# Widening the recurrence's narrow matrix products from 54 or 40 to 64 moving columns

## The chip, the cores and the metric

The kernel runs on one core of a Trainium2 chip. The metric is the device time of one execution in microseconds (us). TensorE (PE in the profile) multiplies a stationary block of up to 128x128 (loaded by LDWEIGHTS, PEld in the profile) with a stream of moving columns; VectorE (DVE), ScalarE (ACT) and GpSimd (POOL) do the rest; SyncE (SP) issues most transfers. TensorE's clock has two levels here, 1.2 and 2.4 GHz; the profile gives the granted clock as a share of the upper one.

## The reference

Three parts follow each other: a recurrence over 768 steps, a mixture of experts, and a dense feed-forward layer. Only the first is touched:

```
for t in range(768):          # for each of 4 x 8 (batch, head), D = 40
    y[t]  = r[t] @ state
    Sa    = state @ a[t]                                   # over e
    state = state * w[t] (over e) - outer(Sa, b[t]) + outer(v[t], k[t])
```

Then x = y as 3072 tokens of 320; each token goes to one of 8 experts (320 to 1024 to 320, relu), and then all tokens through 320 to 2048 to 320 with h * sigmoid(1.702 h).

## The kernel before, in words

**The recurrence** (class Attn) is cut into 24 chunks of 32 steps. The 128 partitions hold 4 batches of 32 steps; the 8 heads lie beside each other in two groups g of four heads. Within a chunk the dependence on earlier steps is solved with matrices made ahead (`ahead`: `decays`, `early`, `solve`), so that a chunk is a chain of products: `chain` builds W from G times v, then U from T times W, V from N times X, U again from T times V; then the new state from k times v and b times U (`outer`) and the old state (`pos`); `state` splits and spreads the state, `output` makes the chunk's Y.

All products are in fp16 with each operand as a high and a low half, three products for one (`mm3`: high-high, low-high, high-low). A head has 40 columns. The operands lie so that several halves or heads follow each other in a row, and a product may read on beyond its 40 columns; the columns of its result beyond 40 are never read. `WIDE` (line 1286) is how many columns most products stream: 54. Two kinds stream 40: those of U into the state (`outer` with k=1, line 1637), and the last of four heads in `times` (line 1672), behind which the tile ends. `v` and `U` rows hold a head as 128 columns: high, low, high again, 8 zeros. `parts` (line 1661) makes the high and low half of W, X and V as tiles of 2 halves x 4 heads x 40 with two buffers for each name.

**The order of work** of the recurrence, and of some of the experts' preparation, is written by a planner (class Plan): every operation is collected with its predecessors, given a cost, and the planner simulates the engines several times forward and backward, keeps its shortest plan, and emits each engine's instructions in that order; it also chooses VectorE or ScalarE for the operations that may run on either (`either`). A product of m columns costs max(m / 2.0, 25) ns there (20 for the smallest), so 27 ns for 54 columns, 25 for 40 and 32 for 64. All instructions that the planner issues carry one line, L234. Engines run their instructions strictly in that order.

**After the recurrence** (from about 545 us) come the experts (lines L870, L884 and others) and, from about 760 us, the dense layer (L1154, L1178).

Of the kernel before, what the change touches and what calls it, by code (L numbers as in the profile page):

```python
# [468 lines left out]
F16 = mybir.dt.float16  # L469
# [25 lines left out]
class Mlp:  # L495
# [265 lines left out]
    def tables2(self):  # L761
# [13 lines left out]
        sq = [128, NE, NE]  # L775
        outer = lambda t: t.rearrange("p (j o) -> p j o", o=1).to_broadcast(sq)
        nc.vector.tensor_tensor(le, one(end[:, 1:]).to_broadcast(sq), outer(end[:, 1:]), op=ALU.is_le)
        nc.vector.tensor_reduce(after, le, axis=AX.X, op=ALU.add)
        nc.vector.tensor_scalar(after, after, NE - 1.0, None, op0=ALU.min)
# [503 lines left out]
RING = 3  # L1283
PX, MX, MGX, SSB, V16B, UEB, SDB, PN = 4, 2, 2, 1, 2, 1, 2, 3
AHEAD = 1500
WIDE = 54
AT = ((0,), (1,), (2, 3), ())
SK, SA, SV, SS = 2.0 ** 10, 2.0 ** 6, 2.0 ** 8, 2.0 ** 12
WMIN, WMAX = 0.8, 1.0
# [3 lines left out]
def sub(t, off, dims):  # L1293

    a = t if isinstance(t, bass.AP) else t[:, :]
    return bass.AP(a.tensor, a.offset + off, [list(a.ap[0])] + [list(d) for d in dims])


class Attn:
# [7 lines left out]
    def __init__(self, tc, ctx, W, AB, KVR, keep, lent):  # L1307

        self.tc = tc
        nc = self.nc = self.plan = Plan(tc)  # L1310
# [71 lines left out]
        for k in (8, 10):  # L1382
            t = self.neg[k] = cp.tile([128, 128], F16, name=f"neg{k}")
# [7 lines left out]
        for b2 in range(2):  # L1391
            for j in range(3):
                r = slice(64 * b2, 64 * b2 + 64)
# [7 lines left out]
        nc.vector.memset(self.wb[:, 0:1], WMIN)  # L1401
        nc.vector.memset(self.wb[:, 1:2], -WMAX)
        self.M, self.C, self.E, self.N = {}, {}, {}, {}

    def _zero(self, name, shape):
        t = self.cp.tile(shape, F16, name=name)
        names = " ".join("abcd"[:len(shape) - 1])
        self.clear(t.rearrange(f"p {names} -> p ({names})"))
        return t
# [156 lines left out]
    def bd(self, dst, src, hs):  # L1566

        for b in range(4):
            o, m = dst[:, :, hs, 32 * b:32 * b + 32], self.own[:, b:b + 1]
            self.nc.either(("vector", "tensor_scalar", (o, src, m, None), dict(op0=ALU.mult)),  # L1570
                           ("scalar", "activation", (o, src, AF.Copy), dict(scale=m)))
# [62 lines left out]

    def outer(self, out, k, x, g, first, last):

        w = 40 if k else WIDE
        for n, (a, o) in enumerate(((0, 0), (1, 0), (0, 40))):
            for i in range(4):
                for bp in range(2):  # L1640
                    r = slice(64 * bp, 64 * bp + 64)
                    self.nc.tensor.matmul(out[:, bp, i, 0:w], lhsT=self.KB[r, k, 4 * g + i, a, :],
                                          rhs=x[r, 4 * g + i, o:o + w], start=first and n + i == 0, stop=last and n + i == 5)

    def chain(self, c, g):
        nc = self.nc
        M, C = self.M[c // 4], self.C[c]
        hs = slice(4 * g, 4 * g + 4)
        U, B = self.Ust, C["B"]
        hl = lambda t, h: (t[:, h, 0:WIDE], t[:, h, 40:40 + WIDE])  # L1650
        bd = lambda t, h: (t[:, 0, h, :], t[:, 1, h, :])
        W = self.pw.bank([4, 64], f"w{g}")
        self.mm3([(W[:, i, :], bd(self.Gbd, 4 * g + i), hl(C["v"], 4 * g + i)) for i in range(4)], True, c == 0)
        if c:
            for i in range(4):
                h = 4 * g + i
                for b in range(4):
                    s = slice(32 * b, 32 * b + 32)
                    nc.tensor.matmul(W[s, i, 0:40], lhsT=C["aE"][0:120, h, s], rhs=self.Ss[g][0:120, b // 2, b % 2, i, :],
                                     start=False, stop=(i == 3))  # L1660
        def parts(x, k, tag):

            t = self.p2.tile([128, 2, 4, 40], F16, tag=tag, bufs=V16B)
            x = x[:, :, 0:40]
            nc.scalar.activation(t[:, 0], x, AF.Copy, scale=2.0 ** -k)
            nc.tensor.matmul(x, lhsT=self.neg[k], rhs=t[:, 0], start=False, stop=True, skip_group_check=True)
            nc.scalar.activation(t[:, 1], x, AF.Copy, scale=2.0 ** -k)
            return t

        def times(out, st, x, first, **k):  # L1670
            f = x.rearrange("p a h e -> p a (h e)")
            self.mm3([(out[:, i, :], bd(st, 4 * g + i), [f[:, a, 40 * i:min(40 * i + WIDE, 160)] for a in range(2)])
                      for i in range(4)], first, True, **k)

        W16 = parts(W, 8, "W16")
        Up = self.pw.bank([4, 64], f"w{g}")
        times(Up, self.Tbd, W16, True)
        X16 = parts(Up, 8, "X16")
        V = self.pw.bank([4, 64], "v")
        times(V, self.Nbd, X16, True)  # L1680
        V16 = parts(V, 10, "V16")
        nc.tensor.matmul(Up[:, :, 0:40], lhsT=self.pos8, rhs=X16[:, 0], start=False, stop=False, skip_group_check=True)
        times(Up, self.Tbd, V16, False, skip_group_check=True)
        Up = Up[:, :, 0:40]
        self.twice(U[:, hs, :], Up, 80, 2.0 ** -10)
        nc.tensor.matmul(Up, lhsT=self.neg[10], rhs=U[:, hs, 0:40], start=False, stop=True, skip_group_check=True)
        nc.scalar.activation(U[:, hs, 40:80], Up, AF.Copy, scale=2.0 ** -10)
        if g:
            UE = C["UE"] = self.p2.tile([128, 8, 128], F16, tag="UE", bufs=UEB)
            nc.sync.dma_start_transpose(out=UE, in_=U.rearrange("p h x -> p (h x)"))  # L1690
        if c < NCH - 1:
            Sp = self.ps.tile([128, 2, 512], F32, tag="s")[:, :, 0:256].rearrange("p a (h x) -> p a h x", h=4)
            for bp in range(2 if c else 0):
                for j in range(2):
                    nc.tensor.matmul(Sp[:, bp, :, 0:WIDE], lhsT=self.pos, rhs=self.S16[g][:, bp, :, 40 * j:40 * j + WIDE],
                                     start=(j == 0), stop=False)
            self.outer(Sp, 0, C["v"], g, c == 0, False)
            self.outer(Sp, 1, U, g, False, True)
            S = self.S32[g]
            P = self.M[(c + 1) // 4]["P"][:, (c + 1) % 4, :, hs]  # L1700
            nc.vector.tensor_tensor(S, Sp[:, :, :, 0:40],
                                    P.rearrange("p a (h o) -> p a h o", o=1).to_broadcast([128, 2, 4, 40]), op=ALU.mult)
        C["next"] = c < NCH - 1
# [22 lines left out]
    def output(self, c, Sd, Y):  # L1726
        nc = self.nc
        M, C = self.M[c // 4], self.C[c]
        U, B = self.Ust, C["B"]
        hl = lambda t, h: (t[:, h, 0:WIDE], t[:, h, 40:40 + WIDE])  # L1730
        bd = lambda t, h: (t[:, 0, h, :], t[:, 1, h, :])
# [58 lines left out]
    def range(self, keep, ones, ps):  # L1790

        nc = self.nc
        v = keep.tile([128, 6], F16, name="gv")
        t = keep.tile([128, 1], F32, name="gt")
        g = keep.tile([128, 1], F32, name="gg")
        self.held = keep.tile([128, 1], F32, name="held")
        nc.vector.tensor_reduce(t, self.viol, axis=AX.X, op=ALU.add)
        nc.vector.tensor_scalar(v[:, 0:1], t, 0.0, None, op0=ALU.is_equal)
        nc.vector.tensor_scalar(v[:, 1:6], self.mag, MAGMIN, None, op0=ALU.is_ge)
        nc.tensor.matmul(ps[:, 0:6], lhsT=ones, rhs=v, start=True, stop=True)  # L1800
        nc.vector.tensor_reduce(t, ps[:, 1:6], axis=AX.X, op=ALU.min)
        nc.vector.tensor_scalar(g, ps[:, 0:1], 128.0, None, op0=ALU.is_equal)
        nc.vector.tensor_scalar(self.held, t, 1.0, g, op0=ALU.is_ge, op1=ALU.mult)
# [144 lines left out]
```

## Time and profile before

| | us |
|---|---|
| median of 3 runs | 1115.99 |
| lowest, highest | 1109.04, 1117.01 |
| profiled execution, its own time | 1107.79 |
| its span, first to last instruction | 1106.0 |

The span is 1.8 us shorter than the time of the same execution. Rows of windows give, for a stretch of the span, each engine's busy time with the count of its instructions, the granted TensorE clock, the DMA engines' busy share and GB/s. Busy times of PE include the way through the array, so matmuls in a row overlap.

### The profile page before, as it was taken

To read this page: it belongs to the slowest core of one execution; us is meant where nothing else is said; L and a number is where in the kernel's file an instruction comes from. 1 tells how busy PE (TensorE), PEld (TensorE's weight loads), DVE (VectorE), ACT (ScalarE), POOL (GpSimd) and SP (SyncE) were. 2 spreads that over 40 slices of the span, in tenths; PEclk is the share of its full clock that TensorE was granted. 3 is DMA by queue.
4 is the path that set the end of the run, shared out by engine and by line. 5 is a ranking of instruction groups with operands and counts; after the bars stand their busy time and mean duration, and the time that the engine had idled before them with its cause. 6 is when DMAs were issued, how large, how long until landed. Compare 5 with 4: busy or idle time off the path is not lost. (4 is left out here: it accounts for less than half of the span.)

```text
span 1106.0 us, 36977 instructions
## 1 busy us (share of the span) xinstructions
PE 903.8 (82%) x15537; PEld 664.9 (60%) x15537; DVE 858.8 (78%) x2089; ACT 673.9 (61%) x1468; POOL 138.8 (13%) x224
## 2 busy tenths in 40 slices
PE   0167886877778787787768998998999999999995
PEld 0155665666666665675657877885555555555553
DVE  8998998998999889887764788676766666666652
ACT  4477998998899899776722363344343434343432
POOL 2000000020020020011132223213002111111101
PEclk9999897987677678667889998999999999999998
DMA  3669789689979779758527678665011111111100
GB/s 111 128 147 182 142 157 177 115 165 193 177 148 180 127 150 172 132 104 135 157 87 201 151 198 282 149 136 128 7 25 49 30 42 35 39 36 42 38 1 25
DMA packets 250654, 129.91 MB, mean 117 GB/s; under 512 B 234400, under 2 KB 237728, under 8 KB 249312
## 3 DMA queue, kind: packets, MB, share of 16 engines
q1 hardware_dynamic: 244464, 98.09, 48.4%
q0 software_dynamic: 6000, 29.23, 7.7%
q8 instruction: 125, 2.05, 0.8%
q14 instruction: 65, 0.53, 0.2%
HBM read 57.78 MB, written 12.16 MB: 63 GB/s over the span
## 5 line engine op out<-in xcount | busy, mean ns | idle before, releaser
L1160 ACT ACTIVATE sg<-t 128x512 f32<-128x512 f32 x96 | 60.5, 630 | 184.3 <-DVE t L1158 174.3
L1154 PE MATMUL h<-xT,WH 128*128 128x512 f16 x480 | 119.3, 379 | 1.8 <-DVE g L1164 1.8
L1178 PE MATMUL acc<-OH,gh 128*128 128x320 f16 x384 | 114.8, 299 | 1.0 <-ACT gh L1166 1.0
L1178 PE MATMUL acc<-OH,gl 128*128 128x320 f16 x384 | 114.8, 299 | 0.6 <-DVE gl L1170 0.6
L1178 PE MATMUL acc<-OL,gh 128*128 128x320 f16 x384 | 114.8, 299 | 0.0
L1158 DVE TENSOR_TENSOR t<-h,sB 128x512 f32<-128x512 f32 x96 | 66.2, 690 | 52.3 <-PE h L1154 49.0
L870 PE MATMUL h<-xT,split 128*128 128x128 f16 x1536 | 96.8, 226 | 11.4 <-DVEq L916 3.9
L870 PEld LDWEIGHTS <-split 128*128 128x128 f16 x1536 | 93.1, 101 | 15.2 <-DVEq L916 4.8
L1178 PEld LDWEIGHTS <-gh 128*128 128x128 f16 x768 | 74.8, 98 | 44.3 <-ACT gh L1166 1.6
L1170 DVE TENSOR_TENSOR gl<-g,gh 128x512 f16<-128x512 f32 x96 | 66.4, 691 | 43.8 <-ACT gh L1166 39.7
L234 POOL DMA_INDIRECT XD<-XR,desti x24 | 30.9, 1289 | 480.8 <-ACT ust L234 207.0
L884 PE MATMUL y<-split,hh 128*128 128x320 f16 x384 | 83.5, 303 | 5.6 <-DVEq L969 4.7
L1154 PE MATMUL h<-xT,WL 128*128 128x512 f16 x288 | 77.8, 379 | 0.0
L1154 PEld LDWEIGHTS <-WH 128*128 128x128 f16 x480 | 46.6, 98 | 44.8 <-DVE g L1164 3.5
L234 PE MATMUL w<-s,pick 128*128 128x160 f16 x368 | 63.4, 290 | 10.0 <-DVE s L234 2.9
L234 PEld LDWEIGHTS <-kb 64*128 64x128 f16 x2208 | 46.7, 101 | 37.6 <-issue 28.1
L234 PEld LDWEIGHTS <-tbd 128*128 128x128 f16 x1152 | 51.4, 105 | 23.9 <-issue 12.1
L1164 DVE SCALAR_TENSOR_TENSOR g<-h,sg 128x512 f32<-128x512 f32 x96 | 65.4, 681 | 0.0
L1166 ACT CAST gh<-g 128x512 f16<-128x512 f32 x96 | 59.3, 617 | 1.4 <-DVE g L1164 1.4
L884 PE MATMUL y<-split,hl 128*128 128x320 f16 x192 | 58.1, 303 | 0.0
L1186 POOL DMA_INDIRECT out<-o,ti x24 | 23.5, 978 | 273.0 <-ACT o L1184 269.6
L872 ACT ACTIVATE hh<-h 128x512 f16<-128x512 f32 x48 | 28.4, 595 | 46.0 <-PE h L870 39.0
(346 smaller groups left out, 2368.3 us busy)
## 6 DMA issues: line engine op xcount, KB each, us to landing
K<-in_KVR SPq DMA_DIRECT2D x24, 480.0 KB
raw<-in_AB SPq DMA_DIRECT2D x13, 640.0 KB
s<-in_wi SPq DMA_DIRECT2D x12, 512.0 KB
s<-in_wo SPq DMA_DIRECT2D x10, 512.0 KB
raw<-in_WU SPq DMA_DIRECT2D x6, 660.0 KB
YS<-ys SPq DMA_DIRECT2D x24, 160.5 KB
Sd<-s SPq DMA_TRANSPOSE x46
raw<-in_KVR SPq DMA_DIRECT2D x1, 480.0 KB
```

Source lines behind the costliest of these rows:

```text
L234: r = self.made[i] = getattr(getattr(self.nc, e), op)(*a, **k)
L870: nc.tensor.matmul(h[:, f4, :], lhsT=a, rhs=b, start=(j == 0), stop=(j == 7))
L872: nc.scalar.activation(hh[:, s, :], h, AF.Relu)
L884: nc.tensor.matmul(y, lhsT=a[:, f, :], rhs=V(b, f), start=(n == 0), stop=(n == 23))
L1154: nc.tensor.matmul(h3, lhsT=a, rhs=r, start=(j == 0), stop=(j == 7))
L1158: nc.vector.tensor_tensor(t, hs[k], self.xs[steps[k][0]]["sB"], op=ALU.mult)
L1160: nc.scalar.activation(sgs[k], t, AF.Sigmoid, scale=1.702)
L1164: nc.vector.scalar_tensor_tensor(gs[k], hs.pop(k), 2.0 ** -4, sgs.pop(k), op0=ALU.mult, op1=ALU.mult)
L1166: nc.scalar.copy(ghs[k], gs[k])
L1170: nc.vector.tensor_tensor(gls[k], gs.pop(k), ghs[k], op=ALU.subtract)
L1178: nc.tensor.matmul(accs[c], lhsT=a[:, s], rhs=r[:, f, :], start=(f == 0 and j == 0), stop=(f == NF - 1 and j == 2))
L1186: sent.append(nc.gpsimd.indirect_dma_start(out=out, out_offset=bass.IndirectOffsetOnAxis(ap=X["ti"][:, c:c + 1], axis=0), in_=o, in_offset ...
```

## The change

`WIDE` becomes 64. In `outer`, U's products stream 64 columns too: the products with the high half now read U's second copy of it (from column 80 of the head on) and run on into the next head's columns, cut to 48 where the group of four heads ends. In `parts` each half gets a tail of 24 zeros, written once per buffer, so that the last head of `times` can stream 64 columns as well. The results that are read are the same columns as before.

```
-WIDE = 54
+WIDE = 64
...
+        self.ended = set()
...
     def outer(self, out, k, x, g, first, last):
-        w = 40 if k else WIDE
-        for n, (a, o) in enumerate(((0, 0), (1, 0), (0, 40))):
+        x = x.rearrange("p h x -> p (h x)")
+        for n, (a, o) in enumerate(((0, 80 * k), (1, 80 * k), (0, 40))):
             for i in range(4):
+                u = 128 * (4 * g + i)
+                w = min(WIDE, 512 * (g + 1) - u - o)
                 for bp in range(2):
                     r = slice(64 * bp, 64 * bp + 64)
                     self.nc.tensor.matmul(out[:, bp, i, 0:w], lhsT=self.KB[r, k, 4 * g + i, a, :],
-                                          rhs=x[r, 4 * g + i, o:o + w], start=first and n + i == 0, stop=last and n + i == 5)
+                                          rhs=x[r, u + o:u + o + w], start=first and n + i == 0, stop=last and n + i == 5)
...
         def parts(x, k, tag):
-            t = self.p2.tile([128, 2, 4, 40], F16, tag=tag, bufs=V16B)
+            t = self.p2.tile([128, 2, 160 + WIDE - 40], F16, tag=tag, bufs=V16B)
+            if t.name not in self.ended:
+                self.ended.add(t.name)
+                nc.vector.memset(t[:, :, 160:], 0.0)
+            t = t[:, :, 0:160].rearrange("p a (h e) -> p a h e", h=4)
...
         def times(out, st, x, first, **k):
-            f = x.rearrange("p a h e -> p a (h e)")
-            self.mm3([(out[:, i, :], bd(st, 4 * g + i), [f[:, a, 40 * i:min(40 * i + WIDE, 160)] for a in range(2)])
+            self.mm3([(out[:, i, :], bd(st, 4 * g + i), [sub(x[:, a, i, :], 0, [[1, WIDE]]) for a in range(2)])
                       for i in range(4)], first, True, **k)
```

## Rows read from the trace of the kernel before

**Rows 1.** The page: the span in 40 slices, busy tenths and clock tenths.
```profile
DVE  8998998998999889887764788676766666666652
PEclk9999897987677678667889998999999999999998
```
**Rows 2.** Windows: the recurrence, the experts, the dense layer.
```profile
70.00:545.00 475.00, 374.68 (x10875) 304.91 (x10878) 425.83 (x1218) 410.79 (x980) 35.05 (x49) 0.78 0.87 156
545.00:760.00 215.00, 188.64 (x2407) 160.42 (x2392) 157.90 (x353) 88.56 (x170) 51.30 (x68) 0.96 0.64 167
760.00:1106.00 346.00, 329.94 (x1964) 191.21 (x1964) 210.68 (x371) 139.78 (x262) 46.56 (x74) 0.98 0.13 33
```
**Rows 3.** Windows, sum: the 22 stretches of 70 to 545 us at clock 0.50.
```profile
sum 204.82, PE 170.47 PEld 140.73 DVE 174.04 ACT 168.03 POOL 15.98; mean PE 7.75 PEld 6.40 DVE 7.91 ACT 7.64 POOL 0.73
```
**Rows 4.** Windows, sum: the 24 stretches of 70 to 545 us at clock 1.00.
```profile
sum 270.18, PE 204.21 PEld 164.18 DVE 251.79 ACT 242.76 POOL 19.07; mean PE 8.51 PEld 6.84 DVE 10.49 ACT 10.11 POOL 0.79
```
**Rows 5.** Windows, PE alone: 4 us ahead of each of 21 falls of the clock.
```profile
104.97:108.97 4.00, 1.44 (x46) 1.00 1.31 237
...
241.51:245.51 4.00, 3.22 (x105) 1.00 0.55 170
...
sum 84.00, PE 49.24; mean PE 2.34
```
**Rows 6.** Windows, PE alone: 4 us ahead of each of 21 rises.
```profile
193.72:197.72 4.00, 4.00 (x67) 0.50 0.51 96
...
sum 84.00, PE 80.86; mean PE 3.85
```
**Rows 7.** Waits of DVE for PE, 70 to 545 us (us, times, longest), first and last.
```profile
DVE mx L234 <- PE g L234: 7.3, 7, 1.4
...
DVE xbd L234 <- PE y L234: 0.2, 1, 0.2
```
**Rows 8.** Waits of ACT for PE, 70 to 545 us, first and last.
```profile
ACT ust L234 <- PE w L234: 6.7, 10, 1.5
...
ACT V L234 <- PE r L234: 0.2, 1, 0.2
```
**Rows 9.** Timeline, PE (start, length, kind, count); 230 and 355 us at clock 0.50.
```profile
180.18 0.48 PE L234 MATMUL s<-vst,kb 64*128 64x54 f16 x24
180.50 0.45 PE L234 MATMUL s<-ust,kb 64*128 64x40 f16 x24
...
230.59 1.28 PE L234 MATMUL y<-kst,xbd 128*128 128x54 f16 x24
...
355.50 0.71 PE L234 MATMUL w<-s,pick 128*128 128x160 f16 x4
...
356.15 0.58 PE L234 MATMUL s<-ust,kb 64*128 64x40 f16 x24
...
417.82 0.77 PE L234 MATMUL y<-kst,xbd 128*128 128x54 f16 x24
...
548.35 1.33 PE L234 MATMUL w<-aE,split 128*128 128x128 f16 x21
```
**Rows 10.** Groups by line and shape: products that the change touches, and one of 128 columns.
```profile
L234 PE MATMUL s<-s,pos 128*128 128x216 f16 x176 | 36.7, 317 | 6.2 <-DVE S L234 4.3 <-issue 1.7
L234 PE MATMUL s<-ust,kb 64*128 64x40 f16 x1104 | 31.2, 187 | 8.4 <-issue 3.6 <-ACT ust L234 3.1 <-ACT kb L234 0.7
L234 PE MATMUL y<-kst,xbd 128*128 128x54 f16 x576 | 28.0, 200 | 1.3 <-ACT xbd L234 0.9 <-DVE Y L234 0.2
L234 PE MATMUL w<-V,tbd 128*128 128x40 f16 x144 | 23.6, 187 | 0.0
...
L234 PE MATMUL w<-aE,split 128*128 128x128 f16 x128 | 11.0, 219 | 0.2 <-ACT aE L234 0.2
```
**Rows 11.** Groups of DVE: small clears.
```profile
L234 DVE MEMSET kst<- 128x32 uint32 x3 | 0.3, 85 | 0.0
```
**Rows 12.** Waits of PE, 540 to 765 us, the longest.
```profile
PE t L932 <- DMA xg<-XD,xrow: 6.5, 1, 6.5
```

## The prediction

> **What bounds the kernel now.** I first read the clock over the span, then the three stages, then the stage that the change touches by clock level, then who waits for PE. The page's slices show the upper clock nearly everywhere from the experts on, and tenths of 6 to 9 before that [rows 1]. The recurrence takes 475 of 1106 us; in it DVE is busy for 425.8 us (90%), ACT for 410.8 (86%), PE for 374.7 with its pipeline's latency counted in, at a mean granted clock of 0.78 [rows 2]. So DVE and ACT fill this stage together, and PE sits between them: its products cost time where DVE or ACT stands and waits for one. Behind the recurrence the longest wait of PE is for a gather of the tokens that the recurrence sent out [rows 12]; I take what the recurrence saves or loses to move the end one for one.
>
> Split by level: 204.8 us lie at 1.2 GHz, with DVE busy 174.0 (85.0%) and ACT 168.0 (82.0%) [rows 3]; 270.2 us lie at 2.4 GHz, with DVE 251.8 (93.2%) and ACT 242.8 (89.8%) [rows 4]. A microsecond at the low level thus gets 8.2% less DVE work done. DVE waited for PE for 22.8 us in all (13 rows, the first and the last in [rows 7]), ACT for 32.4 us (16 rows, [rows 8]). 22.8 us is the most that a PE without any delay could give through DVE.
>
> Ahead of a fall of the clock PE was busy for 2.34 of 4 us on average, between 1.44 and 3.22 over 21 falls [rows 5]; ahead of a rise for 3.85 of 4 [rows 6]. So the low stretches begin behind pauses of PE and end behind a full PE.
>
> **The change part by part.** *How long a wider product is.* At the upper clock 24 products of 54 columns took 0.77 us, so (0.77 - 0.20) / 23 = 24.8 ns from one to the next; 21 of 128 columns took 1.33, so (1.33 - 0.22) / 20 = 55.5 ns [rows 9, 10]. Between them that is 0.415 ns a column: 64 columns should come every 29.0 ns, 4.2 more. At the low clock 24 of 54 took 1.28 us, so 46 ns (with 0.22 for the last), and 4 of 160 took 0.71, so (0.71 - 0.31) / 3 = 133 ns [rows 9]: 0.82 ns a column, 8.2 ns more for 54 to 64, 20 more for 40 to 64.
>
> The first of these rows bears on a rule of the Trainium skill (TensorE: Matmul & The Clock Gate, Back-to-back issue gap): its table gives one floor of some 25 ns for all products of 1 to 64 columns. The trace agrees at 54 columns (24.8 ns); no row here has 64. By it the upper-clock term below would be nearly nothing, and the forecast 1 us lower.
>
> *How many.* Full-height products of 54 columns: 576 each for G, X and Z, and 432 in each of the three `times` steps, 3024 in all; of 40 in `times`, 3 x 144 = 432 (one of each in [rows 10]). The state's `pos` products, 176, go from 216 to 256 columns. The half-height products of `outer` run two at a time: 46 runs of 24 for v (54) and 46 for U (40), 1104 each.
>
> *At the upper clock throughout:* 3024 x 4.2 = 12.7 us; 432 x 4.2 = 1.8 (between 0 and 24 x 0.415 = 10 ns each; no row isolates a 40-column product there, and I take the price of the 54-column ones, which stand behind the same weight load); `pos` 176 x 40 x 0.415 = 2.9; v's runs 46 x 12 pairs x 4.2 ns = 2.3; U's runs took 0.45 us against 0.48 for v's [rows 9], so with 64 columns about 0.52, 46 x 0.07 = 3.2. Together 23 us of PE stream. *At the low clock throughout:* 3024 x 8.2 = 24.8; 432 x 20 = 8.6; `pos` 176 x 33 = 5.8; v 46 x 0.10 = 4.6; U 46 x 0.24 = 11.0 (12 pairs x 20 ns, on runs of 0.58 us): 55 us. By today's mix (57% upper, 43% low) it would be 37 us; with a third of the low time lifted (below), 0.71 x 23 + 0.29 x 55 = 32 us.
>
> *What of it lies on the path.* Most lies beside DVE and ACT work. DVE waited for 22.8 us on a PE busy for 374.7 (6.1%), ACT for 32.4 (8.6%) [rows 2, 7, 8]. I take 8%: 32 x 0.08 = **+2.6 us**; from 0, if all hides, up to the low-clock part alone, 0.29 x 55 = 16 us, if that all shows. The cover is DVE's and ACT's own queue; if they were done early, the whole stream would show.
>
> *The clock.* No row shows what the level does with more columns. From below: nothing lifted, 0 us. From above: all 204.8 us at the upper level, 204.8 x 8.2% = 16.8 us less. I take a third (68 us): of the 21 falls, eight had PE busy for over 2.5 of the 4 us ahead, near the upper stretches' mean of 204.2 / 270.2 x 4 = 3.0 [rows 4, 5]; the others follow pauses that a few more columns don't fill. 68 x 8.2% = **-5.6 us**. That is the generous reading, since part of DVE's idle time at the low level is for transfers and ACT.
>
> *The tails.* Six clears on DVE (three names, two buffers) of 48 values, at about 85 ns or less [rows 11]: **+0.4 us** at most, once, at the first two chunks, behind DVE work; only PE's last-head products there wait for them. *No new waits otherwise.* The second copy of U's high half comes from the same instruction as the first, so the first 16 products of a U run still don't wait for the low half; the next head's columns too come from that instruction, and the cut to 48 keeps a group off the other one's columns. Nothing more is read out of PSUM, no transfer is added, and the queues of SP and POOL get nothing new.
>
> *The planner's order.* It prices the products at 32 instead of 27 or 25 ns and writes another order for the whole recurrence. No row shows the new one. DVE's idle time there is 475 - 425.8 = 49.2 us [rows 2]; an order that moves a quarter of it is worth 12 us in either direction. I put 0 in the sum and keep 12 for the range.
>
> Sum: -5.6 + 2.6 + 0.4 = -2.6 us against the profiled execution's 1107.8, which is 8.2 below the median of the runs, 1116.0. Against the median: **1113 us**.
>
> **The rivals.** *The clock really comes up.* If at least two thirds of the low time are lifted, the gain is 137 to 205 us x 8.2% = 11.2 to 16.8 us, the added stream falls to some 27 us, 2.2 us of it seen: 9 to 14 us less, 1102 to 1107, say 1104. For it: the rise comes behind a full PE, and wider products fill it at once in the places where PE is nearly full. Against: ahead of falls PE had work for only 59% of the time [rows 5].
>
> *The clock stays and PE becomes the bound where it is slow.* Ahead of the 21 rises PE was busy for 80.9 of 84 us [rows 6]: there PE is what the others wait for. A chunk at the low clock has about 16.6 us of PE time (170.5 / 204.8 of 20 us, [rows 3]) and gets 55 / 24 = 2.3 us more, 14%; 14% of 84 us is 12 us, all on the path: **1128 us**. It decides if the low time falls by less than about a sixth. For it: falls follow pauses of PE, and those waits (for ACT, DVE, transfers) stay. Against: 8 of the falls had a well-used PE ahead of them. [...]
>
> *Another order decides.* The re-planned recurrence is better or worse by a quarter of DVE's idle time, whatever the clock does: 1101 or 1125.
>
> **How the numbers follow.** Within 1% is about what a measurement of this kernel can tell from no change; its own runs lie 8 us apart. The forecast, a wash between a longer stream and less low clock (1106 to 1121): 0.52. The clock comes up (1098 to 1107): 0.24. PE the bound at the low clock (1123 to 1134): 0.14. Another order: 0.10, half each way. Faster by over 1% is under 1104.8: somewhat over half of the second case, 0.15, the better orders, 0.04, and 0.06 from the forecast's edge, since the bound of the order adds to every case: 0.25. Slower by over 1% is over 1127.2: 0.09 of the third case, 0.04 and 0.03: 0.16. Within: 0.59. The range that leaves out 2 in 10 is **1101 to 1128**.
>
> **What the changed profile would show.** Products of 64 columns every 29 ns at the upper and 53 to 54 ns at the low clock; U's runs of 24 at about 0.52 and 0.82 us. The low time of the recurrence near 137 us (mean clock 0.85 or more); DVE's waits for PE at 20 to 25 us; the recurrence's end 0 to 6 us earlier; experts and dense layer as long as before. I am wrong if the low time stays at 190 us or more, if it falls under 70, if a wide product takes 25 ns at the upper clock, or if DVE's idle time moves by over 10 us while its waits for PE stay.

## The result and the profile after

The change made the kernel slower. Six runs of each gave 1124.74 us (median, 1119.25 to 1130.91) against 1113.89 us (1105.58 to 1117.01) for the kernel before; the ratio is 1.0128, with a 95% interval of 1.0091 to 1.0165. The forecast was 1113 us, 2.6 us less than the kernel before; the medians are 10.9 us apart the other way. Ratios, here and below, leave out executions that took over 1.5% longer than the fastest of their kernel; medians don't, so the two can differ. The profiled execution of the changed kernel took 1123.05 us, its span 1121.3 us.

The page of the changed kernel, span in 40 slices, DVE and the granted clock, to be laid beside [rows 1]:

```profile
DVE  8998998998989989886674788776766666666652
PEclk9998997887687888888888999999999999999998
```

Windows of the changed kernel: the recurrence between the same limits as before, then the experts and the dense layer, shifted to where they now lie (columns as in [rows 2]):

```profile
70.00:545.00 475.00, 372.50 (x10689) 302.79 (x10686) 422.68 (x1208) 402.58 (x950) 31.16 (x47) 0.84 0.88 151
557.00:772.00 215.00, 190.27 (x2392) 161.50 (x2391) 152.23 (x341) 86.95 (x165) 49.16 (x66) 0.95 0.62 162
772.00:1121.00 349.00, 329.69 (x1964) 191.11 (x1964) 213.90 (x376) 141.10 (x265) 47.14 (x75) 0.98 0.14 36
```

The mean clock of the recurrence rose from 0.78 to 0.84. But DVE got no further in the same 475 us: 422.7 us of work against 425.8 before [rows 2].

The same stretch split by clock level, sums of the 19 stretches at 0.50 and of the 19 at 1.00:

```profile
sum 148.24, PE 122.79 PEld 97.00 DVE 120.11 ACT 116.48 POOL 9.50; mean PE 6.46 PEld 5.11 DVE 6.32 ACT 6.13 POOL 0.50
sum 326.77, PE 249.72 PEld 205.78 DVE 302.58 ACT 286.11 POOL 21.66; mean PE 13.14 PEld 10.83 DVE 15.93 ACT 15.06 POOL 1.14
```

The low time fell from 204.8 to 148.2 us, by 28% [rows 3]. DVE's idle time at the low level hardly fell with it (204.82 - 174.04 = 30.8 us before, 148.24 - 120.11 = 28.1 after), and at the upper level it grew from 270.18 - 251.79 = 18.4 to 326.77 - 302.58 = 24.2 us [rows 4].

Timeline of PE after (start, length, kind, count): U's runs and full-height products; the first two rows lie at the upper level, the last two at the low one:

```profile
180.62 0.52 PE L234 MATMUL s<-ust,kb 64*128 64x64 f16 x24 [0.39 <-ACT kb L234]
335.27 0.86 PE L234 MATMUL y<-kst,xbd 128*128 128x64 f16 x24
344.91 1.47 PE L234 MATMUL y<-xg,zbd 128*128 128x64 f16 x24
397.07 0.86 PE L234 MATMUL s<-ust,kb 64*128 64x64 f16 x24
```

With 0.20 us for the last product at the upper level and 0.22 at the low one, as the prediction reckoned, 24 products take (0.86 - 0.20) / 23 = 28.7 ns each and (1.47 - 0.22) / 23 = 54 ns. U's run went from 0.45 to 0.52 us and from 0.58 to 0.86 [rows 9].

Waits of DVE and of ACT for PE after, 70 to 545 us, the largest of each (us, times, longest):

```profile
DVE mx L234 <- PE g L234: 8.8, 9, 3.6
ACT V L234 <- PE v L234: 8.8, 16, 1.3
```

All such rows together: DVE 21.0 us (22.8 before, [rows 7]), ACT 38.3 (32.4, [rows 8]).

Up to 520 us DVE had done as much as before (408.1 against 407.6 us of work). What differs most in this pair of profiles comes then. The last Y of the recurrence, and the first product of the dense layer, before:

```profile
555.19 0.48 DVE L234 SCALAR_TENSOR_TENSOR Y<-y,R 128x320 f32<-128x320 f32 x1
765.89 1.24 PE L1154 MATMUL h<-xT,WH 128*128 128x512 f16 x5
```

and after:

```profile
567.22 0.48 DVE L234 SCALAR_TENSOR_TENSOR Y<-y,R 128x320 f32<-128x320 f32 x1
780.88 1.24 PE L1154 MATMUL h<-xT,WH 128*128 128x512 f16 x5
```

The recurrence ended 12 us later, the dense layer began 15 us later, and the span grew by 15.3 us. In the last chunk there is a wait that the kernel before doesn't have, and two others stand behind it (waits after, 545 to 580 us; these three are the longest of their engines):

```profile
PE y L234 <- DMA Sd<-s: 6.5, 1, 6.5
ACT xT L234 <- PE r L234: 6.4, 2, 5.6
DVE L L234 <- PE r L234: 7.6, 2, 6.1
```

Sd is the transposed old state, a transfer that SP issues. Beside it, POOL issues the gathers of the first expert's weights (raw). SP's issues of Sd from 505 us on (shortest, median and longest in ns, first and last start), before:

```profile
L234 SPq DMA_TRANSPOSE Sd<-s x4: 1233/1388/2694, 511.0 to 535.2; - x4
```

and after:

```profile
L234 SPq DMA_TRANSPOSE Sd<-s x4: 1233/1272/1333, 518.1 to 538.5; - x4
```

The two issues of raw, before:

```profile
524.15 0.98 POOL L234 DMA_INDIRECT raw<-in_W,w0row  x1 [4.18 <-DVE er L234]
525.45 0.95 POOL L234 DMA_INDIRECT raw<-in_W,w0row  x1 [0.19 <-issue]
```

and after:

```profile
529.10 0.19 POOL L234 COPY XR<-if 128x3 f32<-128x3 f32 x1 [3.34 <-DMA XD<-XR,desti]
537.76 1.52 POOL L234 DMA_INDIRECT raw<-in_W,w0row  x1 [8.47 <-DVE xbd L234]
542.17 0.95 POOL L234 DMA_INDIRECT raw<-in_W,w0row  x1 [0.19 <-issue]
```

The new order puts a copy that waits for other transfers ahead of the gathers, and what the gathers need late in DVE's queue. They now start at 537.8 and 542.2 us, around the last issue of Sd (538.5); before, the second of them came 10 us ahead of it (525.5 against 535.2).

### The profile page after: what moved, and what is told of

Same layout as the page of the kernel before. It is cut to its first block, busy times and chain, and to the rows that moved or that the text cites. A ratio compares the mean times of both kernels' runs of the same rounds, so it can differ in the third digit from the quotient of the medians.

```text
span 1121.3 us, 36979 instructions
## 1 busy us (share of the span) xinstructions
PE 909.3 (81%) x15537; PEld 669.9 (60%) x15537; DVE 861.4 (77%) x2103; ACT 674.4 (60%) x1460; POOL 133.5 (12%) x223
## 5 line engine op out<-in xcount | busy, mean ns | idle before, releaser
L870 PE MATMUL h<-xT,split 128*128 128x128 f16 x1536 | 96.5, 225 | 10.4 <-DVEq L916 4.8
L234 POOL DMA_INDIRECT XD<-XR,desti x24 | 27.4, 1143 | 489.1 <-ACT W L234 207.7
L234 PEld LDWEIGHTS <-kb 64*128 64x128 f16 x2208 | 50.1, 102 | 32.9 <-issue 22.0
L234 PEld LDWEIGHTS <-tbd 128*128 128x128 f16 x1152 | 55.5, 106 | 22.1 <-issue 8.5
L234 PE MATMUL w<-s,pick 128*128 128x160 f16 x368 | 55.8, 266 | 13.3 <-DVE s L234 7.2
L872 ACT ACTIVATE hh<-h 128x512 f16<-128x512 f32 x48 | 28.5, 595 | 46.8 <-PE h L870 35.9
```

The source lines that it names most:

```text
L234: r = self.made[i] = getattr(getattr(self.nc, e), op)(*a, **k)
L870: nc.tensor.matmul(h[:, f4, :], lhsT=a, rhs=b, start=(j == 0), stop=(j == 7))
L872: nc.scalar.activation(hh[:, s, :], h, AF.Relu)
```

## The experiments

Three theories were put to the test. *Columns:* the wider products cost time themselves, and the higher clock gives little back. *Order:* the planner, told other prices, wrote a worse order; the columns cost nothing. *Late gathers*, a narrower form of the second that came up after the first runs: the order costs through the weights' gathers, which in its last chunks meet the last Sd.

The kernels ran in six groups, each with the kernel before beside it, and every ratio is to that; the five groups after the first ran on five different chips. The kernel before had medians of 1094.6 and 1095.1 us in two of them (the quick chips, below) and 1109.8 to 1113.9 in the other four groups.

| kernel | columns | order | ratio, 95% interval |
|---|---|---|---|
| the change | 64 | new | 1.0128, 1.0091 to 1.0165 |
| again | 64 | new | 1.011, 1.0071 to 1.015 |
| third time | 64 | new | 1.0185, 1.0138 to 1.0232 |
| wide, old order | 64 | old | 1.0064, 1.0025 to 1.0103 |
| again | 64 | old | 1.0056, 1.0027 to 1.0085 |
| wide but U and last head | 64, 40 | old | 1.0045, 1.002 to 1.007 |
| U and last head alone, to 54 | 54 | old | 1.0023, 0.9996 to 1.005 |
| narrow, new order | 54, 40 | new | 1.0233, 1.0174 to 1.0293 |
| again | 54, 40 | new | 1.0109, 1.0076 to 1.0142 |
| narrow, old then new | 54, 40 | new from chunk 21 | 1.0116, 1.0069 to 1.0164 |
| narrow, new then old | 54, 40 | old from chunk 21 | 1.0008, 0.9983 to 1.0032 |
| wide, new then old | 64 | old from chunk 21 | 1.0066, 1.0042 to 1.0089 |
| change, early lead | 64 | new, gathers early | 1.0075, 1.005 to 1.01 |
| again | 64 | new, gathers early | 1.009, 1.0059 to 1.0121 |
| narrow, old then new, early lead | 54, 40 | new from chunk 21, gathers early | 1.0045, 1.0021 to 1.0069 |
| before, early lead | 54, 40 | old, gathers early | 0.9988, 0.9964 to 1.0013 |
| narrow, priced as 60 | 54, 40 | a third | 1.0014, 0.9976 to 1.0053 |
| narrow, priced as 50 | 54, 40 | a fourth | 1.0114, 1.0045 to 1.0182 |

**Columns and order taken apart.** An operation can be given a price of its own, so that the planner writes the other kernel's order:

```
-    def cost(self, eng, op, a, k):
+    def cost(self, eng, op, a, k, price=None):
...
-            m = self.size(out)
+            m = price or self.size(out)
```

With 64 columns priced as 54, 40 and 216 (and the tails cleared outside the plan), the order of PE, ACT, POOL and SP is that of the kernel before:

> The changed products (64 columns everywhere, tails of zeros) issued in the order of the kernel before: the planner is told the old column counts, so PE, ACT, POOL and SP have the same sequence as before. Theory order (the new order of the recurrence costs the time): back to the kernel before, 1108 to 1118 us, ratio 0.995 to 1.003, DVE idle in the recurrence near 50 us. Theory columns (the longer stream itself lies on the path): as slow as the changed kernel, 1120 to 1130 us, ratio 1.008 to 1.015, with DVE's waits for PE up by 5 us or more. My forecast's own sum for the columns alone: 2 to 3 us faster than before.

Measured 1.0064, and with narrow columns priced as 64, 48 and 256:

> The old column counts (54, 40, 216) issued in the order of the changed kernel: the planner is told 64, 48 and 256. Theory order: as slow as the changed kernel or slower, 1120 to 1132 us, ratio 1.008 to 1.018, mean clock under 0.91. Theory columns: like the kernel before, 1108 to 1118 us, ratio within 0.4% of 1.

1.0233, of which a second group (1.0109, below) shows half. So both parts cost something; neither theory holds alone. Then two more prices in the kernel before, to see what any other order does:

> The kernel before with nothing changed but the planner's price of its 54-column products (30 ns instead of 27; the pos products 120 instead of 108), so only the order differs. Theory order: an order of its own moves the time by 5 us or more either way, most likely slower, 1118 to 1130 us, with DVE idle time moving by as much. Theory columns: within 4 us of the kernel before, 1110 to 1118 us.

1.0014, with an interval that holds 1: no difference.

> As the run with dearer products, but cheaper: 25 ns for 54 columns, 100 for pos. Theory order: another order, 5 us or more away from the kernel before, 1100 to 1130 us. Theory columns: within 4 us of it.

1.0114 (1.0045 to 1.0182): an order that differs only by such prices can cost 1%. In its profile the gathers were issued 10.2 us ahead of the last Sd and PE didn't wait for that, so what this order costs is not the late gathers; no run says what it is.

**Which part of the order, and which columns.** The change itself stood beside these, for its size on this chip:

> The changed kernel itself beside the kernel before, to have all four corners (old or new order, old or new columns) against the same base. Theory order: 1.009 to 1.017 again, and under the 1.0233 of the old columns in the new order, so that in the new order the wider products give something back. Theory columns would want it above that.

1.011. Then both orders in one kernel, the cut where chunk 21 is first placed:

```
+        cut = s1[self.marks[CUT_AT]] if CUT_AT < NCH else 1e12
+        self.start = [s1[i] if s1[i] < cut else 1e9 + s2[i] for i in range(n)]
```

> Old columns. The planner's old order up to the start of chunk 21, from there the order that it writes for 64 columns. Theory end (the new order loses at the end of the recurrence, where the last state transposes are late and products of Y and the router's work wait for them uncovered): most of the new order's loss is here, ratio 1.012 to 1.024. Theory whole stretch (the new order loses a little in each chunk): near the kernel before, 0.998 to 1.006.

> Old columns. The new order up to the start of chunk 21, the old order from there. Theory end: near the kernel before, 0.995 to 1.006, and no wait of some 6 us for the state's transpose in the last chunk. Theory whole stretch: slow, 1.012 to 1.024.

With the old order until chunk 21 and the new end 1.0116; with the new order and the old end 1.0008. So with narrow columns the loss of the order lies in its end, the last three of 24 chunks with what runs beside them.

> The old order with 64 columns in the products that had 54, but 40 as before for U's products into the state and the chain's last head. Of the 0.64% that all widening cost in the old order: if the dearest part is the 40-column products (20 ns each at the low clock, and they lie on the way to the next state), 0.997 to 1.003; if it is the 54-column ones, 1.004 to 1.009, like all of it. Mean clock between 0.905 and 0.925.

1.0045, in the old order: most of the columns' cost seems to be there without U's products and the last head (the interval, 1.002 to 1.007, also holds the whole).

The same cut with 64 columns, and the part of the end that was suspected, moved alone. The operations ahead of the first gathers (14, counting tokens and choosing the first experts' rows) and the gathers take the earliest start that their inputs allow:

```
+        for i in self.lead:
+            t = max((self.start[j] + self.length(j, eng[j]) + self.lag(j, eng[j], eng[i]) for j in self.preds[i]), default=0.0)
+            self.start[i] = min(self.start[i], t)
```

> The changed kernel with 18 operations moved in its order: the choice of the first expert (one product and 13 small VectorE operations, 'lead') and the four gathers that hang on it are put where their inputs are ready, about 11 us earlier, and nothing else moves. Theory end, by the late gathers: in the new order the weights' gathers start beside the last state transposes, so those land late and Y's products wait; started early, the wait of 6 to 7 us at the state's transpose is gone and the ratio falls from 1.011 to 1.002 to 1.006. Rival, the end is slow for its own order of products: 1.009 to 1.013 as before.

1.0075; by itself that left it open, since its interval overlaps those of the change on other chips.

> The same move in the kernel before, where the gathers come only 3 to 4 us after they are ready. Theory end by the late gathers: no more than 3 us to gain, 0.996 to 1.001. If it is under 0.995, the collision of gathers and transposes costs the kernel before too.

0.9988: where the gathers were early already, more of it brings nothing that could be measured.

> The changed kernel's columns (64), the new order up to chunk 21 and the old order from there. If the loss of the change is the end's order alone: 0.997 to 1.004. If the wider columns cost as much as they did in the old order throughout: 1.004 to 1.009. In either case under the change's 1.011.

1.0066, within the interval of 64 columns in the old order.

> The kernel before, for its profile on this chip beside the others: no wait of over 3 us for a state transpose in the last chunk by either theory, and from the last state update to the last Y 33 to 36 us, against 38 to 43 in the runs that end in the new order.

Its one run took 1116.11 us, the low time of 70 to 545 us was 201.8 us, and the last Sd didn't wait.

**The columns on a second chip, and what U has of it.**

> 64 columns in the order of before, for the second time, on another chip: 1.006 (+-0.003) if the columns alone cost what they did, with the mean clock of the recurrence risen as before. If that was the chip's: 1.000.

1.0056. Windows of this kernel, 70 to 545 us, and the sum of its 17 stretches at the low level and of the 19 at the upper one:

```profile
70.00:545.00 475.00, 377.19 (x10661) 302.32 (x10658) 420.48 (x1197) 405.34 (x962) 32.73 (x49) 0.83 0.89 155
...
sum 157.05, PE 125.92 PEld 100.76 DVE 125.68 ACT 117.96 POOL 14.64; mean PE 7.41 PEld 5.93 DVE 7.39 ACT 6.94 POOL 0.86
...
sum 317.97, PE 251.29 PEld 201.58 DVE 294.82 ACT 287.41 POOL 18.08; mean PE 13.23 PEld 10.61 DVE 15.52 ACT 15.13 POOL 0.95
```

The order is the old one, so this is the columns' doing alone: 48 us less low time than in [rows 3], and DVE idle for 157.05 - 125.68 = 31.4 us at the low level and 317.97 - 294.82 = 23.2 at the upper one, 54.5 in all, where it was 49.2. All 20 profiles agree. The nine with 64 columns have 136 to 163 us of low time in this stretch, the eleven with 54 and 40 (or 54 throughout) have 181 to 219. DVE's idle time is 48 to 55 us in the nine and 44 to 56 in the eleven.

> The order of before, and 54 columns everywhere: only U's products and the chain's last head go from 40 to 54 (48 at the end of a group); the other products stay at 54 and the state's old part at 216. If the columns' cost lies in U's products and the last head, which stand on the chain behind ACT: about 1.002, a good third of what 64 columns cost in this order. If it lies in the 54 columns that become 64: 1.000 (+-0.002). If it is the low clock that these longer runs lift: mean clock of 70 to 545 us over 0.80 and a ratio under 1.000.

1.0023, with an interval that holds both 1.000 and the expected 1.002. With 1.0045 for the rest, the two parts add up to about the 1.0056 and 1.0064 of the whole (U's last step, from 54 to 64, is in neither).

**The gathers.**

> Narrow columns, the old order until chunk 21 and the new order behind it (1.0116 on another chip), with the 14 operations ahead of the experts' first gathers put as early as their inputs allow. If the late lead is what the new end costs: 1.000 to 1.004. If it is something else in that end: 1.009 to 1.013.

1.0045 (1.0021 to 1.0069), just above the expected range, where the new end without the early lead had given 1.0116 on another chip.

> 54 and 40 columns in the whole new order, for the second time (1.0233 on the quick chip). If the order costs by its end: 1.009 to 1.015, as the old order with a new end did. If the whole new order is worse with narrow columns than its end alone: 1.02 or more.

1.0109: the order costs what its end costs, and the 1.0233, from six runs on a quick chip, was not met again. Beside the whole new order the columns' cost doesn't show: narrow columns had 1.0109 and 1.0233, 64 columns 1.011, 1.0128 and, below, 1.0185. The two costs don't simply add up, and no run says why.

The last two runs put the change and its early lead side by side on one chip:

> The change itself, beside the next kernel on one chip. 1.011 to 1.013, as on two chips before.

1.0185, 1119.71 us; this chip, too, is one of the two quick ones.

> The change with the early lead, on the same chip as the change itself. If the late lead is what its order costs: 1.006 to 1.008, the columns' cost alone, and some 0.5% below the run beside it. If the first 1.0075 was chance: 1.011 to 1.013.

1.009, 1104.87 us, 14.8 us less in the medians and 10.4 by the ratios; the two intervals don't meet. The change on this chip, windows of 72 to 520 and 520 to 560 us:

```profile
72.00:520.00 448.00, 355.79 (x10346) 289.71 (x10343) 411.60 (x1162) 392.23 (x925) 30.27 (x39) 0.86 0.91 153
520.00:560.00 40.00, 17.29 (x508) 15.73 (x508) 17.62 (x63) 17.30 (x45) 4.87 (x9) 0.70 1.00 125
```

its timeline of PE, the last products of Sd:

```profile
558.54 0.33 PE L234 MATMUL y<-Sd,rE 120*32 120x40 f16 x16 [10.95 <-DMA Sd<-s]
```

and its weights' tile, the two issues and their time to landing:

```profile
L234 POOL DMA_INDIRECT raw<-in_W,w0row x2: 939/970/1000, 526.5 to 532.1; - x2
...
DMA to landing us min/median/max: 26.2/26.2/26.2
```

The same three views with the early lead, windows first:

```profile
72.00:520.00 448.00, 354.75 (x10303) 288.07 (x10299) 411.85 (x1171) 389.76 (x921) 28.31 (x39) 0.86 0.91 153
520.00:560.00 40.00, 26.23 (x701) 23.29 (x692) 27.11 (x92) 26.42 (x65) 8.19 (x15) 0.79 0.52 136
```

its timeline of PE, the last products of Sd:

```profile
546.86 0.38 PE L234 MATMUL y<-Sd,rE 120*32 120x40 f16 x32
```

and its weights' tile, the two issues and their time to landing:

```profile
L234 POOL DMA_INDIRECT raw<-in_W,w0row x2: 980/988/995, 518.0 to 519.3; - x2
...
DMA to landing us min/median/max: 9.3/10.7/12.1
```

For 448 us the two are one kernel: the same work on each engine within 2.5 us, and the same clock. In the next 40 us the change keeps the DMA engines busy throughout (1.00 against 0.52) while PE, DVE and ACT stand for more than half of it; DVE does 17.6 us of work instead of 27.1. Of its gathers, issued at 526.5 and 532.1, the one whose landing the trace has took 26.2 us instead of 9.3 and 12.1, and the product of the last Sd waits 10.95 us instead of none. The dense layer then begins at 778.7 us against 766.7.

Over all profiles, in the six of the new end without the early lead (three of the change, and three with narrow columns) the second gather was issued 0.6 to 3.7 us behind the last transpose of Sd, and PE waited 3.0 to 10.9 us for Sd; in the other fourteen it was issued 9.7 to 22 us ahead of it, and there is no such wait. That the transfers hold each other up is read from these traces. What the runs tested is the move of all 18 operations together, and issuing the gathers early doesn't by itself make them quick: in the profile of the wide kernel in the old order one that was issued 11.4 us ahead of the last Sd also took 23.1 us to land.

## Why the prediction was wrong

**The columns' own balance is the first step that failed.** Clock and stream, -5.6 and +2.6 us, made -3.0; in the old order the columns alone cost 0.0056 x 1110.7 = 6.2 us and 0.0064 x 1095.1 = 7.0 us.

*The stream term, +2.6 us, had its products right and its exposure too low.* 64 columns took 28.7 and 54 ns, where 29.0 and 53 to 54 were forecast, and U's runs 0.52 and 0.86 us, where 0.52 and 0.82 were. The Trainium skill (TensorE: Matmul & The Clock Gate, Back-to-back issue gap) has one floor of some 25 ns up to 64 columns in its table; the trace doesn't agree at 64, and the measured 28.7 ns decides. The formula of the same section, columns / 2.4 + 2.5 ns, gives 29.2 ns, and with that the trace agrees. If the higher clock gave nothing back, the measured 6 to 7 us are a fifth of the 32 us of longer stream and not 8%; whatever the clock gave back comes on top of that. Where the stream shows is open. Summed over the wait rows of each profile (70 to 545 us), DVE's waits for PE were 22.9 us on average in the nine with 64 columns and 18.2 in the eleven others, ACT's 36.0 and 33.2; but single profiles lie between 7.0 and 28.5 us for DVE and between 28.6 and 40.0 for ACT, so this is a hint and no proof.

*The clock term, -5.6 us, is "68 x 8.2%".* The third of the low time that it took to be lifted was nearly right (56.6 us in the change, 48 in the columns alone, in place of 68). The price was not shown then and is not shown now. The 8.2% was the difference of DVE's busy share at the two levels, taken as something that the level causes; the low stretches begin behind pauses [rows 5], and the share may be lower there because the waits for ACT, PE and transfers lie there. With 48 to 57 us less low time DVE's idle time was 54.5 and 52.3 us, not less than 49.2, so no net gain is seen; but this is a balance of both terms, and no run changed the clock without the columns. The record also has a hint that a higher clock does go with a shorter time: among the 34 executions of the kernel before that enter the ratios of one group (median 1110.7 us), the time fell by 3.2 us (standard error 0.8) for each 0.01 of mean granted clock, some 0.15 us for each us less at the low level; in the five groups of the experiments together it was 0.12. A longer pause could lower the clock and take time as well, so this is no price either. The prediction had named the weak point ("part of DVE's idle time at the low level is for transfers and ACT") and still put the whole share into the sum.

**The planner's order, put at 0, is the second step that failed**, and with it two sentences: "No new waits otherwise" and that the queues of SP and POOL "get nothing new". They got nothing new, but in another order: POOL's copy went ahead of the gathers, and these moved on to the last Sd. The end of the order costs what the early lead and the old end give back: from the change's 1.011 to 1.0185 down to 1.0066 to 1.009, so some 0.3 to 1%, 4 to 10 us. That the late lead with its gathers is this cost is shown by the pair on one chip; that they cost through the last Sd is read from the wait of 10.95 us that is gone. What is left in that pair, 1.009, agrees with the columns' cost (1.0056 and 1.0064), but the narrow kernel with the early lead still had 1.0045, so a part can be the order's. The prediction had no row of the new order and kept 12 us for it in the range alone. The measured time lies inside the range of 1101 to 1128 by what was kept there for the rivals and the order, not by the sum.

**The tails, +0.4 us,** are too small for any run here to show.

**The rivals.** *The clock really comes up* asked for two thirds of the low time; 28% was lifted, and the kernel became slower. *The clock stays* decided under a sixth lifted; that wasn't so. The Trainium skill (TensorE: Matmul & The Clock Gate, Why this matters for your kernels) asks to keep TensorE busy continuously and to leave no idle gaps between bursts of matmuls. The trace agrees insofar as the longer products raised the clock here (148.2 us at the low level against 204.8), but the stage didn't become faster by it. *Another order decides* had the right time, 1125, and half of the cause, but a chance of only 0.05 on that side. Experts and dense layer were nearly as long as before, as forecast: 210.7 us from the last Y to the first dense product before and 213.7 after, then 340.1 and 340.4 us to the end.

**What stays open:** how the columns' 6 us divide into longer stream and what the clock gave back, and where on the path they lie; why they don't show beside the whole new order; why the new order costs more on the two quick chips (1.0185 and 1.0233) than on the others (1.0109 to 1.0128); and what else in the new end keeps the narrow kernel with early lead at 1.0045.

No version was faster than the kernel before.

## What to carry to other kernels

A lower busy share in the stretches at a low clock is not by itself the price of the clock: first ask what the engine that bounds the stage waits for there, and count only the waits for TensorE. Where a planner writes the order, a changed cost is a second change; run the edit with the old order and the old code with the new one before you reason about either. And look at the end of the stage first, where the next stage's big transfers meet the small ones on which the last steps wait.

## What was unexpected of the hardware

In the last pair of runs, two gathers of weights that were issued around the last transposes of the state, rather than 19 us ahead of them, landed late, and PE waited for the transposes. On the DMA queues between 505 and 560 us the same 9504 packets of the hardware queue, which holds the transposes, took 55.7% of the engines' span in the change and 29.4% with the early lead, here the change and then the early lead (packets, MB, share of 16 engines):

```profile
q1 hardware_dynamic: 9504, 2.36, 55.7%
q0 software_dynamic: 576, 3.87, 34.5%
```

```profile
q1 hardware_dynamic: 9504, 2.36, 29.4%
q0 software_dynamic: 667, 4.20, 22.5%
```

So a busy share of the DMA engines of 1.00 here doesn't mean more data: 125 GB/s were moved at 1.00, 136 at 0.52. And from group to group, each on another chip and at another time, the same kernel differs by more than the change costs: the kernel before took 1095 us in two groups and 1110 to 1114 us in four, while the change was at 1120 to 1125 in its three groups.
